# The first MLP layer of the last two token groups in seven products instead of eight, with partial sums in the reopened score banks

## The chip, the cores and the metric

The kernel runs on one core of a Trainium2 chip. The metric is the device time of one execution in microseconds (us); the kernel before takes 329.04 us, the median of three runs (328.96 to 329.2). TensorE is called PE here, its weight loads PEld, VectorE DVE, ScalarE ACT, GpSimd POOL and SyncE SP.

## The reference

Attention with 16 extra keys ("beacons") is followed by a two-layer MLP over its output:

```python
# q, k, v: (8, 8, 576, 64); beacon_k, beacon_v: (8, 8, 16, 64)
scores = q @ concat(beacon_k, k).T / sqrt(64)      # causal over k; the beacons are always seen
a = softmax(scores)
x = (a @ concat(beacon_v, v)).transpose(0, 2, 1, 3).reshape(4608, 512)
h = x @ w_in                                       # 512 -> 2048
g = h / (1 + exp(-1.702 * h))
out = g @ w_out                                    # 2048 -> 512
```

## The kernel before, in words

**Attention.** The 64 pairs of batch and head go in 16 sets of four heads (two sets to a batch). For each set a DVE transpose brings q and k into place (line 418), PE forms scores in chunks of 512 columns for four heads (line 447), which fill one tile of four PSUM banks named s, ACT takes the exponential into a 16-bit tile E (line 458; E has three buffers), POOL or DVE masks (lines 479, 472), DVE sums the exponentials (line 497), PE multiplies E by the values (line 534), and DVE normalises into xT (lines 546 to 569). xT holds the MLP's input transposed: 512 features as four blocks of 128 partitions, by tokens.

**MLP.** The 4608 tokens go in ten groups: two of 256 tokens, then eight of 512 (groups 2 to 9). For a group of 512, the first layer (`e_m1`, line 593) makes 16 tiles of 128 hidden features by 512 tokens. Each tile is four matmuls with 512 columns, summed over the four feature blocks, in one PSUM bank. ACT then takes each tile through the gated activation into a 16-bit tile g (`e_gelu`, line 614). The second layer of groups 2 to 9 already goes by the seven-product scheme (`products`): with 2x2 blocks, seven block products replace eight. DVE makes sums of blocks of g (`e_s`, through `add`, line 658; sixteen operations a group), PE forms the seven products, each 32 matmuls with 256 columns (`e_prod`, line 707), and ACT (`e_half`, line 718) and DVE (`e_join`, line 723, seven a group) put the products together into the output tiles osb, which SP stores (line 730). The weight sums that this needs are made once (`e_t`, line 658, into tB and into a quarter of w2).

**PSUM.** Four of the eight banks belong to s. The other four are a ring, tiles u0 to u3, that serves the value products, the first layer and the second layer. A tile of the ring is free for its next use when the operation that `closes` it has read it.

**Order.** Every piece of work is an operation with an engine, a duration and dependencies, entered by `plan.op`. The order on each engine is written out by hand in the table `ORDER`, as numbers of operations. `Plan.run` walks that table with the entered durations to choose a bank for each ring tile and to merge the engines' orders into one program. On the chip each engine takes its instructions in that order and waits on semaphores, so the entered durations set which bank a tile gets, not when it runs.

Of the kernel before, what the change touches and what calls it, by code (L numbers as in the profile page):

```python
# [10 lines left out]
ALU = mybir.AluOpType  # L11
# [7 lines left out]
        170, 173, 176, 145, 125, 148, 150, 177, 182, 188, 191, 227, 194, 197, 232, 183, 203, 234, 200, 178, 237,  # L19
        179, 206, 258, 241, 209, 184, 263, 185, 212, 265, 213, 248, 246, 268, 214, 215, 401, 251, 253, 272, 218,  # L20
        404, 275, 244, 279, 219, 220, 407, 282, 284, 277, 221, 414, 320, 296, 304, 290, 302, 292, 300, 298, 312,
        308, 294, 318, 314, 310, 306, 316, 426, 435, 423, 343, 338, 339, 340, 433, 431, 438, 344, 345, 359, 349,
        341, 464, 346, 350, 351, 352, 354, 574, 355, 429, 360, 361, 577, 356, 362, 357, 372, 365, 583, 474, 477,
        373, 366, 374, 367, 605, 480, 484, 375, 482, 607, 368, 506, 502, 488, 492, 610, 490, 486, 498, 504, 500,
        508, 514, 510, 516, 494, 496, 512, 534, 593, 596, 535, 536, 539, 540, 550, 541, 542, 537, 742, 545, 546,
        547, 548, 603, 745, 551, 552, 553, 599, 601, 619, 622, 748, 555, 556, 557, 558, 561, 755, 625, 627, 629,
        562, 563, 776, 568, 564, 569, 570, 571, 779, 764, 767, 659, 637, 641, 657, 649, 651, 647, 661, 635, 631,
        653, 805, 772, 770, 774, 643, 655, 633, 639, 645, 679, 680, 815, 818, 700, 681, 682, 684, 701, 915, 690,
        685, 686, 691, 692, 702, 918, 687, 693, 695, 703, 696, 924, 821, 823, 697, 698, 706, 946, 825, 707, 713,
        708, 709, 948, 934, 937, 714, 715, 716, 827, 951, 944, 940, 942, 853, 831, 833, 855, 857, 851, 843, 835,  # L30
        837, 847, 839, 845, 829, 849, 841, 1083, 960, 963, 875, 876, 880, 877, 878, 881, 882, 1086, 968, 966, 970,
        883, 1089, 902, 909, 903, 886, 891, 1096, 887, 888, 889, 892, 893, 1117, 904, 894, 905, 896, 897, 1120, 898,
        899, 910, 911, 1105, 1108, 1146, 912, 976, 994, 996, 972, 978, 1000, 992, 982, 974, 998, 990, 984, 988, 980,
        1002, 986, 1256, 1156, 1113, 1111, 1115, 1159, 1025, 1020, 1026, 1021, 1259, 1022, 1027, 1031, 1023, 1028,
        1265, 1164, 1162, 1166, 1041, 1042, 1287, 1036, 1047, 1032, 1048, 1033, 1037, 1038, 1034, 1039, 1289, 1054,
        1055, 1049, 1056, 1043, 1044, 1050, 1292, 1057, 1198, 1172, 1168, 1178, 1184, 1180, 1194, 1170, 1174, 1176,
        1275, 1278, 1182, 1186, 1196, 1188, 1190, 1281, 1301, 1285, 1283, 1304, 1216, 1217, 1221, 1192, 1222, 1227,
        1218, 1223, 1228, 1219, 1224, 1232, 1229, 1233, 1230, 1307, 1311, 1309, 1237, 1327, 1333, 1238, 1243, 1234,
        1244, 1235, 1323, 1239, 1245, 1250, 1251, 1341, 1240, 1246, 1252, 1253, 1337, 1405, 1315, 1331, 1343, 1411,
        1335, 1321, 1403, 1431, 1313, 1325, 1407, 1419, 1317, 1423, 1425, 1319, 1339, 1421, 1409, 1329, 1361, 1413,  # L40
        1366, 1382, 1429, 1362, 1363, 1401, 1367, 1364, 1427, 1368, 1383, 1372, 1369, 1373, 1374, 1375, 1388, 1377,
        1389, 1378, 1390, 1395, 1379, 1384, 1380, 1385, 1391, 1396, 1415, 1397, 1398, 1470, 1454, 1417, 1455, 1449,
        1471, 1450, 1451, 1476, 1452, 1456, 1477, 1457, 1478, 1460, 1461, 1462, 1463, 1465, 1466, 1467, 1468, 1472,
        1479, 1473, 1483, 1484, 1485, 1486,
# [3 lines left out]
        195, 198, 233, 235, 201, 204, 238, 180, 207, 259, 210, 264, 186, 266, 269, 216, 402, 405, 408, 222, 417,  # L48
        415, 297, 291, 303, 305, 301, 299, 293, 309, 321, 295, 319, 313, 315, 311, 307, 317, 436, 439, 342, 465,
        468, 575, 578, 584, 587, 606, 608, 503, 507, 489, 491, 493, 487, 499, 505, 509, 515, 517, 495, 501, 511,  # L50
        497, 513, 611, 538, 743, 746, 749, 756, 758, 777, 780, 660, 642, 638, 652, 658, 648, 650, 636, 632, 662,
        654, 806, 644, 634, 656, 640, 646, 809, 916, 683, 919, 928, 925, 947, 949, 952, 828, 832, 854, 856, 852,
        858, 834, 838, 844, 840, 836, 846, 830, 848, 850, 842, 1084, 879, 1087, 1090, 1099, 1097, 1118, 1121, 1147,
        1150, 977, 995, 979, 997, 993, 973, 975, 983, 991, 999, 989, 1001, 981, 1003, 985, 987, 1257, 1260, 1024,
        1269, 1266, 1288, 1290, 1293, 1199, 1179, 1173, 1181, 1185, 1195, 1171, 1169, 1175, 1177, 1183, 1187, 1197,
        1189, 1191, 1193, 1220, 1328, 1334, 1324, 1342, 1316, 1332, 1344, 1406, 1412, 1338, 1336, 1404, 1432, 1314,
        1408, 1420, 1318, 1424, 1326, 1426, 1320, 1340, 1422, 1410, 1330, 1322, 1414, 1430, 1402, 1365, 1428, 1416,
        1418, 1453,
# [3 lines left out]
        123, 163, 160, 124, 224, 169, 128, 166, 172, 175, 146, 147, 126, 149, 151, 225, 226, 398, 190, 193, 196,  # L62
        199, 255, 256, 257, 202, 205, 286, 242, 411, 287, 211, 208, 243, 399, 249, 247, 400, 250, 412, 254, 252,
        273, 245, 274, 280, 276, 413, 281, 285, 283, 278, 289, 461, 288, 462, 419, 580, 420, 463, 326, 327, 328,
        421, 322, 92, 323, 324, 422, 427, 428, 424, 425, 325, 330, 334, 329, 335, 432, 336, 331, 434, 337, 332, 333,
        470, 347, 582, 353, 471, 581, 472, 430, 473, 358, 363, 475, 476, 478, 479, 481, 485, 739, 483, 369, 376,
        370, 589, 752, 740, 590, 615, 518, 753, 921, 519, 754, 526, 591, 527, 520, 528, 592, 529, 521, 741, 522,
        597, 523, 594, 530, 595, 598, 531, 802, 532, 524, 533, 616, 543, 525, 604, 549, 617, 618, 554, 600, 620,
        602, 623, 624, 621, 559, 760, 628, 761, 762, 626, 630, 565, 763, 566, 768, 572, 765, 811, 812, 766, 803,
        804, 769, 773, 771, 671, 1080, 775, 672, 813, 922, 663, 814, 664, 675, 667, 816, 673, 819, 668, 669, 817,  # L70
        923, 665, 666, 820, 674, 676, 677, 1093, 670, 688, 694, 678, 930, 822, 824, 699, 931, 826, 932, 933, 704,
        710, 938, 939, 935, 936, 717, 711, 945, 941, 943, 1081, 956, 957, 958, 871, 1082, 1094, 1095, 959, 872, 873,
        867, 859, 961, 962, 964, 965, 860, 863, 1262, 1143, 861, 874, 862, 868, 864, 967, 865, 971, 866, 969, 884,
        869, 870, 1101, 1144, 890, 1145, 1102, 895, 1103, 1104, 900, 906, 1109, 907, 1110, 913, 1106, 1107, 1152,
        1153, 1004, 1154, 1005, 1155, 1264, 1006, 1263, 1016, 1012, 1017, 1157, 1114, 1112, 1013, 1018, 1116, 1160,
        1008, 1161, 1009, 1019, 1158, 1014, 1015, 1029, 1010, 1165, 1011, 1007, 1163, 1167, 1035, 1040, 1271, 1051,
        1045, 1058, 1052, 1297, 1272, 1273, 1274, 1298, 1299, 1276, 1279, 1300, 1200, 1204, 1280, 1201, 1277, 1205,
        1282, 1302, 1206, 1286, 1284, 1208, 1305, 1209, 1202, 1303, 1210, 1212, 1203, 1306, 1207, 1213, 1225, 1231,
        1308, 1312, 1214, 1310, 1215, 1211, 1236, 1247, 1241, 1248, 1254, 1349, 1345, 1350, 1346, 1347, 1353, 1351,
        1354, 1355, 1356, 1357, 1358, 1359, 1370, 1348, 1360, 1352, 1376, 1381, 1386, 1392, 1393, 1445, 1446, 1433,  # L80
        1399, 1437, 1434, 1438, 1447, 1435, 1441, 1442, 1436, 1443, 1444, 1439, 1448, 1440, 1458, 1464, 1469, 1480,
        1474, 1481, 1487,
    ],
    "POOL": [
        8, 10, 12, 14, 16, 17, 19, 21, 23, 25, 27, 29, 31, 33, 35, 37, 39, 41, 43, 45, 47, 110, 49, 51, 113, 114,
        53, 55, 57, 59, 133, 61, 136, 137, 63, 65, 67, 69, 71, 378, 230, 231, 229, 380, 382, 384, 386, 236, 388,
        390, 392, 239, 240, 394, 396, 261, 260, 262, 441, 443, 270, 267, 271, 449, 451, 453, 455, 457, 459, 403,
# [29 lines left out]
class Plan:  # L117
# [6 lines left out]
    def __init__(self, ring):  # L124
        self.ops = []
        self.ring = ring
        self.tiles = {}
        self.closers = {}
# [76 lines left out]
def kernel(  # L205
# [27 lines left out]
    HF = S // 2  # L233
    NKT = DMODEL // P
    NNT = DFF // P
    RING = 4

    NE, NB2, NB3 = 3, 2, 3

# [893 lines left out]
```

## Time and profile before

| what | value |
|---|---|
| time, median of three runs | 329.04 us |
| span of the profiled execution, first to last instruction | 327.2 us |
| around the span (median less span) | 1.8 us |
| mean granted TensorE clock | 0.999 |
| busy: PE, PEld, DVE | 314.6, 214.7, 237.2 us |
| busy: ACT, POOL | 202.1, 113.9 us |
| line 593, first layer: 704 matmuls | 130.6 us |
| line 707, second layer of groups 2 to 9: 896 matmuls | about 121 us |
| line 614, activation of the first layer: 128 | 70.5 us, 598 ns each |

No time of the profiled execution is listed beside its span, so the median of the runs stands in for it: 1.8 us lie around the span. A matmul's busy time overlaps that of the next one, so the time of a run of matmuls is read from start to start. An ACT or DVE instruction likewise overlaps the next one on its engine by some tens of ns to about 0.1 us. An engine's idle time costs nothing unless another engine is waiting for it.

### The profile page before, as it was taken

To read this page: it belongs to the slowest core of one execution; us is meant where nothing else is said; L and a number is where in the kernel's file an instruction comes from. 1 tells how busy PE (TensorE), PEld (TensorE's weight loads), DVE (VectorE), ACT (ScalarE), POOL (GpSimd) and SP (SyncE) were. 2 spreads that over 40 slices of the span, in tenths; PEclk is the share of its full clock that TensorE was granted. 3 is DMA by queue.
4 is the path that set the end of the run, shared out by engine and by line. 5 is a ranking of instruction groups with operands and counts; after the bars stand their busy time and mean duration, and the time that the engine had idled before them with its cause. 6 is when DMAs were issued, how large, how long until landed. Compare 5 with 4: busy or idle time off the path is not lost.

```text
span 327.2 us, 9966 instructions
## 1 busy us (share of the span) xinstructions
PE 314.6 (96%) x4364; PEld 214.7 (66%) x4364; DVE 237.2 (72%) x480; ACT 202.1 (62%) x236; POOL 113.9 (35%) x178
## 2 busy tenths in 40 slices
PE   6589999999999999999999999999999999999995
PEld 6467665545775477746878878547764776447884
DVE  4838798777987989977998798858558853006674
ACT  1676697678767586679666786868577212674010
POOL 8765478190419312941177019400042000000000
PEclk9999999999999999999999999999999999999999
DMA  7999999293424911792039709500120012000122
GB/s 126 159 201 211 204 186 184 37 123 107 99 72 64 190 34 34 79 198 43 7 53 178 119 4 124 154 2 3 34 98 0 2 34 83 15 0 2 65 98 97
DMA packets 58220, 28.83 MB, mean 88 GB/s; under 512 B 41280, under 2 KB 53568, under 8 KB 58176
## 3 DMA queue, kind: packets, MB, share of 16 engines
q0 software_dynamic: 47552, 18.49, 47.9%
q1 hardware_dynamic: 10560, 9.69, 9.2%
q8 instruction: 34, 0.56, 0.7%
q14 instruction: 10, 0.08, 0.1%
q10 hardware_dynamic: 64, 0.01, 0.0%
HBM read 37.22 MB, written 9.44 MB: 143 GB/s over the span
## 4 chain that ended last, share of the span: by engine, by line
PE 83%; DMA 6%; DVE 4%; POOL 3%; ACT 2%; issue 1%; ACTq 0%; POOLq 0%
PE u L593 34%; PE u L707 30%; PE u L534 9%; PE s L447 7%; PE u L638 3%; DMA w<-in_moe_w_out_dram 3%; DMA w<-in_moe_w_in_dram 3%; ACT E L458 1%; DVE sA L658 1%; DVE g L626 1%; POOL vb L378 1%; POOL w L384 0%; DVE bkn L403 0%; ACT L614 0%; DVE kT L418 0%
## 5 line engine op out<-in xcount | busy, mean ns | idle before, releaser
L593 PE MATMUL u<-xT,w 128*128 128x512 f16 (+1 forms) x704 | 130.6, 341 | 0.6 <-ACT g L614 0.5
L458 ACT ACTIVATE E<-s 128x2048 f16<-128x2048 f32 (+5 forms) x66 | 98.9, 1515 | 44.9 <-PE s L447 44.4
L614 ACT ACTIVATE g<-u 128x512 f16<-128x512 f32 x128 | 70.5, 598 | 53.7 <-PE u L593 53.2
L593 PEld LDWEIGHTS <-w 128*128 128x128 f16 x704 | 67.6, 98 | 54.3 <-issue 1.9
L479 POOL TENSOR_SCALAR_AFFINE_SELECT E<-E 128x512 f16<-128x512 f16 (+3 forms) x78 | 49.3, 665 | 110.8 <-ACT E L458 79.1
L723 DVE SCALAR_TENSOR_TENSOR osb<-u,osb 128x512 f32<-128x512 f32 x56 | 37.3, 683 | 24.5 <-PE u L707 22.5
L707 PEld LDWEIGHTS <-g 128*128 128x128 f16 x512 | 48.3, 98 | 9.3 <-issue 0.2
L707 PE MATMUL u<-w,g 128*128 128x256 f16 x384 | 50.6, 273 | 0.0
L447 PE MATMUL s<-qT,kT 32*128 32x32 f16 (+20 forms) x1376 | 34.6, 228 | 5.7 <-ACT E L458 2.8
L447 PEld LDWEIGHTS <-kT 32*128 32x128 f16 x1376 | 25.2, 92 | 22.5 <-issue 14.4
L707 PEld LDWEIGHTS <-sA 128*128 128x128 f16 x384 | 36.3, 98 | 5.3 <-issue 0.3
L707 PE MATMUL u<-tB,sA 128*128 128x256 f16 x256 | 35.1, 273 | 0.1
L658 DVE TENSOR_TENSOR sA<-g 128x512 f16<-128x512 f16 x32 | 12.9, 416 | 26.2 <-ACT g L614 26.2
L569 DVE TENSOR_TENSOR xT<-u,rz 128x352 f16<-128x352 f32 (+2 forms) x52 | 25.5, 517 | 6.5 <-PE u L534 6.3
L378 POOL DMA_DIRECT2D vb<-in_v_dram x32 | 27.4, 876 | 2.4 <-DMA qn<-in_q_dram 1.6
L534 PE MATMUL u<-E,vb 128*32 128x352 f16 (+8 forms) x928 | 27.4, 262 | 0.0
L497 DVE TENSOR_TENSOR zs<-zs,E 128x1344 f16<-128x1344 f16 (+2 forms) x36 | 22.7, 633 | 5.3 <-POOL E L479 4.4
L534 PEld LDWEIGHTS <-vb 128*32 128x32 f16 (+1 forms) x928 | 19.9, 96 | 5.5 <-issue 1.7
L418 DVE STREAM_TRANSPOSE kT<-kn 128x576 f32<-128x576 f32 x16 | 20.1, 1257 | 2.1 <-DMA kn<-in_k_dram 1.4
L418 DVE STREAM_TRANSPOSE qT<-qn 128x576 f32<-128x576 f32 x16 | 19.9, 1241 | 0.3 <-DMA qn<-in_q_dram 0.3
L546 DVE STREAM_TRANSPOSE zt<-u 128x224 f32<-128x224 f32 (+2 forms) x32 | 15.0, 470 | 5.9 <-PE u L534 5.8
L497 DVE TENSOR_TENSOR zs<-E 128x1856 f16<-128x1856 f16 x12 | 15.8, 1320 | 3.3 <-POOL E L479 3.3
(48 smaller groups left out, 252.3 us busy)
## 6 DMA issues: line engine op xcount, KB each, us to landing
out_dram<-osb SPq DMA_DIRECT2D x36, 256.0 KB, 2.4
kn<-in_k_dram POOLq DMA_DIRECT2D x16, 288.0 KB, 6.9
qn<-in_q_dram POOLq DMA_DIRECT2D x16, 288.0 KB, 6.5
vb<-in_v_dram POOLq DMA_DIRECT2D x24, 128.0 KB, 6.4
w<-in_moe_w_in_dram POOLq DMA_DIRECT2D x8, 256.0 KB, 9.4
w<-in_moe_w_out_dram POOLq DMA_DIRECT2D x4, 512.0 KB, 13.5
vb<-in_v_dram POOLq DMA_DIRECT2D x8, 112.0 KB, 5.0
vb<-in_v_dram POOLq DMA_DIRECT2D x8, 80.0 KB, 7.9
```

The lines of the kernel that those rows point to most:

```text
L378: nc.gpsimd.dma_start(out=t[0 : hi - lo, j, h0:h1, :], in_=v[b, h0:h1, lo:hi, :].rearrange("h n d -> n h d"),)
L418: nc.vector.transpose(out=f32(dst.rearrange("p n e -> p (n e)")).rearrange("p (r t) -> p t r", t=TR), in_=f32(src[:, :]).rearrange("p (t c ...
L447: nc.tensor.matmul(sc[:, h, o : o + w], kT[s % NB2][r : r + 32, j * P : (j + 1) * P, d], qT[s % NB2][r : r + 32, a : a + w, d], start=(d = ...
L458: nc.scalar.activation(out=Es[s][:, :, c0:c1], in_=ss[i][:, :, o : o + c1 - c0], func=AFT.Exp, scale=0.125,)
L479: nc.gpsimd.affine_select(out=blk, in_=blk, compare_op=ALU.is_ge, fill=0.0, base=off + (Nb if j == 0 else 0), pattern=[[0, Q], [1, w]], ch ...
L497: nc.vector.tensor_tensor(out=t, in0=E[:, :, Z0:S] if i == 1 else t, in1=E[:, :, wcol[i] : wcol[i] + S - a], op=ALU.add,)
L534: nc.tensor.matmul(u[32 * h : 32 * h + 32, a:e], lhs, src[0:kw, h, col : col + e - a], start=first, stop=last,)
L569: nc.vector.tensor_tensor(out=xT[:, 2 * hs + x : 2 * hs + x + n, t0 : t0 + w], in0=rings[("av", s, x, half)][:, 0 : n * w].rearrange("p (n ...
L593: nc.tensor.matmul(u[:, o + a - t0 : o + e - t0], w1t[:, kp, nt * P : (nt + 1) * P], xT[:, kp, a % XR : (e - 1) % XR + 1], start=(kp == 0) ...
L614: nc.scalar.activation(out=gts[g][:, n0:n1, 0:w], in_=rings[("m1", g, n0)][:, 0 : n * w].rearrange("p (n w) -> p n w", n=n), func=AFT.Gelu ...
L707: nc.tensor.matmul(u[:, HM * mt : HM * (mt + 1)], lhs[:, n, mt * P : (mt + 1) * P], rhs[:, n, :], start=(n == 0 and mt == 0), stop=(n == H ...
L723: nc.vector.scalar_tensor_tensor(out=osbs[(g, dst)][:, :], in0=rings[("p", g, p)][:, :], scalar=scale_of(g), in1=osbs[(g, src)][:, :], op0 ...
```

## The change

The set `FAST = (8, 9)` names the last two groups. Their first layer no longer goes through `e_m1` and `e_gelu`. `fast` cuts the first layer's weights into 2x2 blocks (256 input features by 1024 hidden features) and the group's tokens into two halves of 256, and works in four steps, called tiles here, of twice two blocks of 128 hidden features. A tile has seven parts, each of four matmuls with 256 columns (`e_part`).

- Block sums: four of the weights, made once (`e_ws`, 2048 columns each; three into a buffer of E that is free by then, one into bkf), and four of the tokens for each group (`e_xs`, 512 columns each, into another buffer of E). All eight kinds are DVE additions through `add`.
- The partial sums that several outputs share are not formed in SBUF: ACT copies a bank to another bank (`e_seed`), and the next parts go on summing on top of the copy. Part 1 goes into bank a. Its copy in bank b takes part 6; the copy of that, in bank e, takes part 5. Bank a then takes part 2, bank b part 4, bank e part 3.
- Part 7 goes into bank f, and ACT copies it to SBUF (`e_keep7`, into the buffers qn and kn, which the last transposes have left). DVE adds it to bank e before part 3, and to bank b after part 4 (`e_sum7`), into SBUF.
- ACT takes the four results of a tile through the activation (`e_gelu4`, 512 columns each): two from PSUM, two from SBUF. So a tile has four activations, as before, and three ACT copies and two DVE additions that are new.

PSUM: the pool of s is closed after the last scores and reopened as four tiles of one bank, u4 to u7, so the ring has eight banks from then on, for the remaining work of group 7 and of attention too. The last exponential must have read s first (`late`). A bank that is to be seeded must have been wholly written by its user before (`seeded`, `partial`).

`ORDER` is the same up to about 100 us before the end; from there on PE, ACT, DVE and POOL have a new one, in which operations of attention, of group 7 and of groups 8 and 9 are moved against each other. The dependencies of the second layer are as before, on two activations for each block instead of one.

```diff
-    RING = 4
+    RING, MORE = 4, 4
...
+            else:
+                if not spare:
+                    scoring.close()
+                    spare.append(
+                        ctx.enter_context(tc.tile_pool(name="psv", bufs=1, space=bass.MemoryType.PSUM))
+                    )
+                rings[key] = spare[0].tile([P, 512], F32, tag=f"u{i}", name=f"u{i}")
...
+    FAST = (8, 9)
...
+        for n in range(2):
+            for x in range(2):
+                nc.tensor.matmul(
+                    u[:, HM * n : HM * (n + 1)],
+                    lhs[:, x, (2 * i + n) * P : (2 * i + n + 1) * P],
+                    rhs[:, x, :],
+                    start=fresh and n == 0 and x == 0,
+                    stop=n == 1 and x == 1,
+                    skip_group_check=not fresh,
+                )
+    def e_seed(src, dst):
+        nc.scalar.mul(out=ring_tile(dst)[:, :], in_=rings[src][:, :], mul=1.0)
...
+    def e_keep7(src, slot):
+        nc.scalar.mul(out=hold[slot], in_=rings[src][:, :], mul=1.0)
+
+    def e_sum7(src, slot, dst):
+        nc.vector.tensor_tensor(out=hold[dst], in0=rings[src][:, :], in1=hold[slot], op=ALU.add)
...
+            p1 = part(1, "a", [], True)
+            c1 = grab("seedb", 490, [p1], lambda: e_seed(key["a"], key["b"]), ring=key["b"])
+            p2 = part(2, "a", [c1])
+            gelu(0, 0, p2, key["a"], key["a"])
+            p6 = part(6, "b", [c1])
+            c2 = grab("seede", 490, [p6], lambda: e_seed(key["b"], key["e"]), ring=key["e"])
+            p7 = part(7, "f", [], True)
+            x7 = grab("keep7.", 480, [p7] + last, lambda: e_keep7(key["f"], slots[0]), closes=key["f"])
+            p5 = part(5, "e", [c2])
+            p4 = part(4, "b", [c2])
+            a1 = grab("sum22.", 605, [p5, x7] + last, lambda: e_sum7(key["e"], slots[0], slots[1]), "DVE")
+            g22 = gelu(1, 1, a1, slots[1])
+            p3 = part(3, "e", [a1])
+            gelu(0, 1, p3, key["e"], key["e"])
+            a2 = grab("sum21.", 605, [p4, x7] + last, lambda: e_sum7(key["b"], slots[0], slots[2]), "DVE", closes=key["b"])
+            g21 = gelu(1, 0, a2, slots[2])
...
+        if g in FAST:
+            fast(g, xs, old)
+            products(g)
+            return
```

## The prediction

> **What bounds the kernel now.** I read the page's busy shares first, then the waits of PE from 222 us on, the stretches of the last 100 us, the chain that ended last, and the timeline around one first-layer tile.
>
> ```profile
> PE 314.6 (96%) x4364; PEld 214.7 (66%) x4364; DVE 237.2 (72%) x480; ACT 202.1 (62%) x236; POOL 113.9 (35%) x178
> PEclk9999999999999999999999999999999999999999
> ```
>
> PE is busy for 96% of the span at full clock. A busy PE need not be a limit, so I look for gaps: the waits of PE after 222 us are an empty list, and the stretches say the same.
>
> ```profile
> 225.00:240.00 15.00, 15.00 (x263) 12.08 (x264) 8.79 (x21) 8.49 (x7) 1.83 (x3) 1.00 0.06 20
> 240.00:265.00 25.00, 25.00 (x301) 15.27 (x300) 19.34 (x43) 12.77 (x19) 4.73 (x7) 1.00 0.13 44
> 265.00:324.00 59.00, 58.38 (x416) 39.76 (x408) 25.40 (x56) 19.55 (x34) 0.00 (x0) 1.00 0.11 40
> ```
>
> The columns are length, then PE, PEld, DVE, ACT and POOL busy, clock, DMA. PE has no idle time from 225 us to its last matmul near 323.4. From 265 us on, where groups 8 and 9 lie, DVE works 25.4 of 59 us and ACT 19.6, so there is room for more work on both. The chain confirms that only PE's own work stands between there and the end:
>
> ```profile
> 274.75 18.99 PE u L593 x88
> ...
> 300.26 8.30 PE u L707 x76
> ...
> 323.42 0.69 DVE osb L723
> ```
>
> These two rows are the prices. A matmul of 512 columns in a run costs 18.99 / 88 = 215.8 ns, one of 256 columns, with its own weight load, 8.30 / 76 = 109.2 ns. After the last matmul come a join, a store and the end of the program.
>
> **What PE loses.** A group's first layer is 64 matmuls of 512 columns: 64 x 215.8 = 13.81 us. After the change it is 4 tiles x 7 parts x 4 = 112 of 256 columns: 112 x 109.2 = 12.23 us. That is 1.58 us a group, **3.16 us** for two. In the two programs' orders of instructions I find these and no other matmuls changed, and as many changes between scores, values and whole-array matmuls as before (16 after 225 us). Each part lasts 0.437 us.
>
> The row for 256 columns comes from operands like the new ones (16-bit, 128x128 weights from SBUF). The Trainium skill, "TensorE: Matmul & The Clock Gate", section "Back-to-back issue gap", speaks against the change: in a stream of load and matmul pairs it gives about 81 ns for 128 columns and 131 ns for 512. Estimated on a line between, 256 columns cost 98 ns, and a group would go from 64 x 131 = 8.4 to 112 x 98 = 10.9 us, 2.6 us more. This case's trace disagrees, with 215.8 and 109.2 ns.
>
> **What ACT and DVE gain.** ACT: as many activations, plus 8 tiles x 3 copies = 24 of 128x512. The rows of that size (line 614, 598 ns; line 718, 597) agree whatever the function; back to back one costs 0.49 us (below). So 24 x 0.49 to 0.60 = 11.8 to 14.4 us, and ACT has 31 to 34 of some 56 us. Sixteen copies write PSUM, and no row shows ACT doing that. The low bound is a write with no fixed part: the exponentials of line 458 take 1877 ns for 2048 columns and 1452 for 1536, so 512 columns alone cost 0.43 us. The high bound is twice the row, 1.20. I take 0.60, the row of the same shape, which differs only in the destination.
>
> DVE: 4 weight sums of 2048 columns, where the row for tB (line 658) has 1214 ns twice and 1695 once: 4.9 to 6.8 us. They fall between 240 and 265, where DVE has 5.7 us idle, 6.2 more from 225 on, and the new order brings three sums of exponentials (633 ns each) forward into the earlier stretch and puts two normalisations (517 ns) after 265. That makes 19.3 + 4.9 - 0.6 x 3 - 1.0 = 21.4 of 25 us, 23.3 at the dear price. It stays under cover. What is late next is the last normalisation of set 15, which the first part of group 8 needs; the fourth weight sum stands just before it. If the cover is gone, 0.5 us a sum, at most 2 us. After 265: 8 token sums (0.34 to 0.42 us) and 16 additions of part 7 (as line 723's 128x512 from PSUM: 0.61 to 0.69), 12.5 to 14.4 us on 25.4, some 39 of 56.
>
> DMAs, SP's order and POOL's work stay; on POOL only masks change places, and it is idle 10 of 15 us there. Six more waits stand on PE, most for beacon loads that landed long ago: a wait instruction lasts 51 ns in the trace, so 0 to 0.3 us. The one between 250 and 255 us left no gap in PE, so I take zero.
>
> **The new waits.** PE runs in order: behind a part that waits for a copy, every later matmul stands, those of the second layer too. What a link costs:
>
> ```profile
> 311.00 1.03 PE L593 MATMUL u<-xT,w 128*128 128x512 f16 x4
> 311.86 1.04 PE L707 MATMUL u<-w,g 128*128 128x256 f16 x8
> 312.06 0.60 ACT L614 ACTIVATE g<-u 128x512 f16<-128x512 f32 x1 [2.01 <-PE u L593]
> ```
> ```profile
> 68.87 1.08 ACT L614 ACTIVATE g<-u 128x512 f16<-128x512 f32 x2
> 69.52 0.59 PE L593 MATMUL u<-xT,w 128*128 128x512 f16 x2 [0.49 <-ACT g L614]
> ```
>
> ACT starts 0.20 us after PE goes on to the next run. In the second view two activations take 1.08, so the second follows at 0.49; the first ends at 69.47 and PE starts at 69.52, 0.05 later. A link PE, ACT, PE is 0.20 + 0.60 + 0.05 = 0.85 us, two parts (0.87). Over DVE it is 0.20 + 0.69 + 0.05 = 0.94. In the new order at least three parts (1.31 us) stand between the two ends of every link: exactly three in 6 of the 40, four or more in the rest. What can still hurt is ACT's own queue: one instruction ahead costs 0.49. I followed the order with these prices through the stretches with least room. The copy of bank b for tile 3 of group 8 must await the part-7 addition of tile 2, which frees its bank: 0.20 + 0.69 + 0.03 + 0.60 + 0.05 = 1.57 us, and four parts (1.75) cover it, 0.18 to spare. The copy into e for tile 2 stands behind an activation that comes late: 0.20 + 0.49 + 0.60 + 0.05 = 1.34 against 1.75. I find none under 0.1. The bound on the dear side: 6 close links x 0.5 = 3 us. I take zero, because each link has been counted.
>
> Eight banks in place of four give nothing: PE had no gap to remove.
>
> **The rivals.**
> 1. **Forecast: PE's work falls and nothing takes its place.** 329.04 - 3.16 = **325.9 us**, span 324.0. Chance 0.70.
> 2. **Waits in the chains or on DVE's weight sums eat part.** ACT copying at 0.8 instead of 0.6 would use up the tightest 0.18, and a few tenths at some five links make 1 to 2 us: 326.9 to 327.9. Against it: the counted margins. Chance 0.17.
> 3. **Slower: copies into PSUM are dear, and PE waits for ACT.** Place: the 16 seeds. With d for one, and some 0.2 us of room on average, the loss is 16 x (d - 0.8): it decides from d = 1.0 us (16 x 0.2 = 3.2), and at the bound of 1.20 it makes 6.4, 332.3 us. For it: no row shows such a write. Against it: the row does not depend on what is written (f16 598, f32 597). Chance 0.09. The Trainium skill, "ScalarE: Activation LUTs", section "Step-by-step: what each stage is for", has ScalarE's writes to PSUM faster than to SBUF; no run here shows it, and by that rule this rival has no chance.
> 4. **Narrow matmuls are bound by their weight loads.** A load is 98 ns busy, a pair 109.2: if the new sources make a pair 123.3 ns, 112 x 123.3 = 13.81 and the gain is gone; one after the other, 98 + 107 = 205 ns, two groups lose 224 x 96 = 21 us, 347. Against it: line 707 runs 896 such pairs with no gap. Chance 0.02; the page on TensorE above is this rival's rule in its milder form, plus 5.2 us.
> 5. **The change doesn't do what it says**: of the two groups only group 8 saves, because in group 9 PE runs short of ready work near the end, where its second layer needs all activations: 329.04 - 1.58 = 327.5. Against it: in the new order 22 product parts (9.6 us) stand behind the last first-layer part, about as now. Chance 0.02.
>
> **How the numbers follow.** Faster by over 0.2% (0.66 us, about what a measurement of this kernel can tell from no change) holds for 1, most of 2 and 5: 0.70 + 0.14 + 0.02 = 0.86. Within 0.2%: 0.03 of 2 and 0.01 of 3, 0.04. Slower: 0.08 of 3 and 4's 0.02, 0.10. The range: 325.3 (0.6 below the forecast for the spread of runs and a price read a little off) to 327.4, which takes in the six waits at 0.3 and losses to 1.5 us, the nearer part of rival 2: 0.68 of case 1 and 0.12 of case 2. The dear bounds (2 us of weight sums, 3 of links, rivals 3 to 5) lie beyond it, with the 0.2 that is left.
>
> **What would show it.** Right: the span 324.0, PE without waits after 225 us, 224 matmuls of 256 columns at 109 ns from start to start, ACT near 33 and DVE near 39 us busy in the last 56. Wrong: PE waiting for the copies (rival 2 or 3), their mean above 0.8 us, or DVE's weight sums running past set 15's normalisation.

## The result, and the profile after

The changed kernel takes **326.18 us** (median of five runs, 325.29 to 326.32) against 329.2 us for the kernel before (five runs, 328.96 to 329.44). The ratio is 0.9906, with a 95% interval of 0.9894 to 0.9918: 3.02 us less. The forecast was 325.9, in a range of 325.3 to 327.4.

The page of the profile after, first the busy shares and the granted clock:

```profile
PE 310.6 (96%) x4460; PEld 223.6 (69%) x4460; DVE 253.2 (78%) x508; ACT 213.7 (66%) x260; POOL 114.1 (35%) x178
...
PEclk9999999999999999999999999999999999999999
```

PE's share stays at 96% and the span is 323.6 us. ACT has 11.6 us more work and DVE 16.0 us more, and PE 4.0 us less. The stretches of the last 100 us, with the columns as before (length, PE, PEld, DVE, ACT, POOL, clock, DMA):

```profile
225.00:240.00 15.00, 15.00 (x282) 11.91 (x276) 9.65 (x21) 9.83 (x7) 3.09 (x5) 1.00 0.06 21
240.00:265.00 25.00, 25.00 (x280) 15.74 (x278) 20.39 (x42) 10.56 (x19) 3.06 (x4) 1.00 0.09 33
265.00:320.00 55.00, 54.40 (x508) 48.36 (x496) 39.99 (x82) 31.76 (x58) 0.00 (x0) 1.00 0.14 48
```

PE is still without a gap until its last matmul. In the last stretch DVE is at 40.0 of 55 us, where it was at 25.4 of 59, ACT at 31.8, where it was at 19.6, and the weight loads fill 48.4. The list of PE's waits after 222 us is empty, as it was. The chain that ended last, from 265 us on (start, length, what):

```profile
270.06 3.49 PE u L813 x32
...
309.79 3.51 PE u L724 x32
313.32 0.60 ACT osb L735
313.93 1.64 issue
315.56 0.70 DVE osb L740
316.35 0.70 DVE osb L740
317.12 0.70 DVE osb L740
317.85 1.35 DVE osb L740 x3
```

Two things are to be seen. A matmul of the new parts costs 3.49 / 32 = 109.1 ns. And the chain no longer ends in PE's last matmul and one join. It leaves PE at 313.3 and ends in a row of DVE's joins. The 1.64 us of "issue" between them are a wait for which the profile names nobody; e8 below shows that it is a wait for PE.

**Where the time went.** Up to about 224 us both kernels issue the same matmuls in the same order, so the start of the matmul that follows the 3300th can serve as a mark in every trace. It divides a span into a part that the change does not touch, the stretch from there to the start of the last matmul, and the end.

| kernel | mark at | from it to the start of the last matmul | from there to the end |
|---|---|---|---|
| before | 221.68 us | 101.43 us | 4.11 us |
| after | 220.96 | 98.17 | 4.46 |
| e1, before with eight banks | 221.98 | 101.32 | 4.11 |
| e2, part 7 twice | 221.45 | 101.66 | 4.47 |
| e3, copies twice | 221.46 | 102.56 | 4.46 |
| e4, weight sums twice | 221.41 | 98.81 | 4.46 |
| e5, copies longer | 221.91 | 98.71 | 4.46 |
| e6, additions twice | 221.80 | 104.53 | 4.46 |
| e7, half of each part | 221.90 | 93.00 | 4.47 |
| e8, one step of the order moved | 221.73 | 98.17 | 4.15 |
| e9, after again | 221.99 | 98.17 | 4.47 |
| e10, e8 again | 223.51 | 98.17 | 4.15 |

The spans differ by 3.6 us (327.2 and 323.6), but 0.72 of that arose in the untouched part, in the first 50 us of it; over all traces that part scatters from 220.96 to 223.51. What the change did is in the other two columns: 3.26 us less in the stretch, 0.35 us more at the end, 2.91 in all. The medians say 3.02.

### The profile page after: what moved, and what is told of

Same layout as the page of the kernel before. It is cut to its first block, busy times and chain, and to the rows that moved or that the text cites. A ratio compares the mean times of both kernels' runs of the same rounds, so it can differ in the third digit from the quotient of the medians.

```text
span 323.6 us, 10241 instructions
## 1 busy us (share of the span) xinstructions
PE 310.6 (96%) x4460; PEld 223.6 (69%) x4460; DVE 253.2 (78%) x508; ACT 213.7 (66%) x260; POOL 114.1 (35%) x178
## 4 chain that ended last, share of the span: by engine, by line
PE 83%; DMA 6%; ACT 3%; POOL 3%; DVE 3%; issue 1%; DVEq 0%; ACTq 0%; POOLq 0%
PE u L724 28%; PE u L610 27%; PE u L551 9%; PE s L464 8%; PE u L813 8%; PE u L655 4%; DMA w<-in_moe_w_out_dram 3%; DMA w<-in_moe_w_in_dram 2%; ACT E L475 2%; DVE osb L740 1%; DVE sA L675 1%; POOL vb L395 1%; POOL w L401 0%; ACT L631 0%; POOL kn L379 0%
## 5 line engine op out<-in xcount | busy, mean ns | idle before, releaser
L610 PE MATMUL u<-xT,w 128*128 128x512 f16 (+1 forms) x576 | 101.9, 332 | 1.1 <-DVE xT L586 0.6
L610 PEld LDWEIGHTS <-w 128*128 128x128 f16 x576 | 55.0, 98 | 41.0 <-issue 2.1
L631 ACT ACTIVATE g<-u 128x512 f16<-128x512 f32 x96 | 51.7, 599 | 21.4 <-PE u L610 21.1
L724 PEld LDWEIGHTS <-g 128*128 128x128 f16 x512 | 48.4, 98 | 7.1 <-issue 0.2
```

Source lines behind the costliest of these rows:

```text
L610: nc.tensor.matmul(u[:, o + a - t0 : o + e - t0], w1t[:, kp, nt * P : (nt + 1) * P], xT[:, kp, a % XR : (e - 1) % XR + 1], start=(kp == 0) ...
L631: nc.scalar.activation(out=gts[g][:, n0:n1, 0:w], in_=rings[("m1", g, n0)][:, 0 : n * w].rearrange("p (n w) -> p n w", n=n), func=AFT.Gelu ...
L724: nc.tensor.matmul(u[:, HM * mt : HM * (mt + 1)], lhs[:, n, mt * P : (mt + 1) * P], rhs[:, n, :], start=(n == 0 and mt == 0), stop=(n == H ...
```

## The experiments

**e1: the banks alone.** The kernel before with its own order, and the score banks reopened as four ring tiles.

```diff
-    FAST = (8, 9)
+    FAST = ()
```
(and `ORDER` of the kernel before in the changed kernel)

> The kernel before, with its own order, but with the score banks reopened as four more tiles of the ring; both layers of all groups as before. Theory 1 (the change gained only the matmul time of the first layer, 3.16 us): PE had no gap after 225 us in the profile of before, so more banks give nothing: within 0.3 us of before. Theory 2 (part of the gain is that PE and ACT no longer share four banks): 1 to 3 us faster than before.

329.09 us against 329.09 of before measured beside it, ratio 1.0002 (0.9992 to 1.0011). The banks alone give nothing that the time can show. The stretch became 0.11 us shorter: in the trace of before, one first-layer matmul at 244.5 starts 0.10 us late, while it waits for its bank, and with eight banks it does not. That gap does not show in the list of waits.

**e2: eight parts instead of seven.**

```diff
-  lambda: e_part(g, p, i, key[at], fresh)
+  lambda: [e_part(g, p, i, key[at], fresh) for _ in range(2 if p == 7 else 1)]
```

> The changed kernel with part 7 formed twice in each of the eight tiles (the second overwrites the first, the result is the same): eight parts instead of seven, 256 matmuls of 256 columns in the two groups instead of 224. Theory 1 (PE's work sets the time): 8 x 4 x 109.2 ns = 3.5 us slower than the changed kernel, 0.3 to 0.5 us slower than before. Theory 2 (banks and order carry part of the gain): as slow, but then faster than before by what they carry, 1 us or more. Theory 3 (ACT or DVE sets the time of these groups): less than 2 us slower than the changed kernel, since PE then has idle time to fill.

329.36 us, ratio to before 1.0013 (1.0003 to 1.0023). The stretch grew by 3.49 us, which is 32 x 109.1 ns. With the eighth product given back, nothing of the gain is left. Against e1, which has the same eight banks, the stretch is 0.34 us longer, and 256 matmuls of 256 columns should take 256 x 109.1 - 128 x 215.8 ns = 0.31 us more than 128 of 512. So in the stretch the new order, the copies and the additions cost PE at most some 0.03 us; what they do cost is the 0.36 at the end. Theory 1 holds, and 2 and 3 fall.

**e3: each copy from bank to bank twice.**

```diff
-        nc.scalar.mul(out=ring_tile(dst)[:, :], in_=rings[src][:, :], mul=1.0)
+        for _ in range(2):
+            nc.scalar.mul(out=ring_tile(dst)[:, :], in_=rings[src][:, :], mul=1.0)
```

> The changed kernel with each of the 16 copies from bank to bank done twice, which adds 0.49 us of ACT to each. Theory 1 (each link between PE and ACT has only some tenths of a us to spare: 0.2 to 0.5 in the tightest places that were counted): the spare time is used up at about ten places and PE waits 0.1 to 0.5 us at each: 2 to 3 us slower than the changed kernel. Rival of the prediction (little to spare, loss of 16 x (d - 0.8) with d = 1.09): 4.6 us slower. Theory 3 (ACT has much room: 32 of 55 us busy): under 0.5 us slower.

330.47 us, ratio 1.0044 (1.0027 to 1.0060): 4.3 us slower than the changed kernel and slower than before. Theory 3 falls. The two other numbers can't be taken as they stand, because the edit added more than 0.49 us to a copy. The first copy from bank to bank, alone in the changed kernel and twice here:

```profile
268.18 0.58 ACT L823 ACTIVATE u<-u 128x512 f32<-128x512 f32 x1 [5.25 <-DVE osb L740]
```
```profile
268.68 1.20 ACT L824 ACTIVATE u<-u 128x512 f32<-128x512 f32 x2 [5.25 <-DVE osb L740]
```

In all 16 pairs the second copy starts 0.61 to 0.65 us after the first, when the first has ended, and not 0.49 after it: a pair takes 1.2 us. For that the rival's rule says 16 x (1.2 - 0.8) = 6.4 us, so its 4.6 came near the measured 4.3 by luck. PE's waits in that kernel:

```profile
PE u L813 <- ACT u L824: 2.7, 8, 0.5
```

The list counts from the modelled end of the matmul before, some 0.16 us after the next could have started. Counted against the same matmuls of the changed kernel, ten new parts start 0.18 to 0.68 us late, 4.4 us in all. In the changed kernel the ten have 0.19 to 0.43 us to spare, and 0.62 less what each has makes 3.1 us. At six of them that agrees with their delay to 0.02. The other four come 0.56 to 0.68 us late instead of 0.21 to 0.37. ACT's timeline shows why at one of them (start, length, operation, count), first in the changed kernel, then here:

```profile
269.70 1.14 ACT L823 ACTIVATE u<-u 128x512 f32<-128x512 f32 x2 [0.95 <-PE u L813]
270.76 0.59 ACT L837 ACTIVATE g<-u 128x512 f16<-128x512 f32 x1
```
```profile
270.61 2.30 ACT L824 ACTIVATE u<-u 128x512 f32<-128x512 f32 x4 [0.73 <-PE u L813]
272.82 0.59 ACT L838 ACTIVATE g<-u 128x512 f16<-128x512 f32 x1
```

Two copies stand one behind the other, so the second bears its own lengthening and that of the first: from the start of the first to the end of the second 2.30 us pass instead of 1.14. The part that needs the second copy had 0.31 us to spare and meets 1.16, not 0.62. Of the 0.85 that are left, 0.18 show at the part that needs the first copy and 0.67 at this one. At the other three it is not shown which lengthening ACT's queue still carried.

**e4: each weight sum twice.**

```diff
-  lambda i=i: e_ws(i)
+  lambda i=i: [e_ws(i) for _ in range(2)]
```

> The changed kernel with each of the four weight sums done twice: 4.9 us more of DVE between 240 and 265 us, where it is busy 20.4 of 25 us. Theory 1 (the sums lie in DVE's idle time, which ends with one set of normalisations): DVE is just full, and PE waits up to 1 us: 0.5 to 1.2 us slower than the changed kernel. Rival (the sums already stand in the way of attention's last normalisations): the whole 4.9 us shows, or more than 2.

326.48 us, ratio 0.9924 (0.9907 to 0.9940), 0.3 us slower than the changed kernel by the medians, 0.64 by the stretch. All of it is at the place that was named, the first parts of group 8 waiting for attention's last normalisation (the second wait, 0.13 us, is below the list's limit):

```profile
PE u L813 <- DVE xT L586: 0.4, 1, 0.4
```

So 5.0 us more of DVE's work (each second sum starts 1.22 to 1.25 us after the first) cost 0.64: the weight sums do lie under cover. The rival falls.

**e5: each copy some tenths longer.**

```diff
+        for w in (64, 512):
+            nc.scalar.mul(out=ring_tile(dst)[:, 0:w], in_=rings[src][:, 0:w], mul=1.0)
```

> The changed kernel with a copy of the first 64 columns ahead of each of the 16 copies from bank to bank, so that each costs ACT some 0.1 to 0.2 us more (0.17 us of fixed part, of which about 0.1 overlaps). In the trace of the changed kernel the shortest time from the end of a copy to the matmul that needs it is 0.24 us, of which 0.05 is the handover. Theory 1 (0.2 us to spare at the tightest link, and the loss of 4.4 us with a whole second copy came from spare time being used up): under 0.3 us slower than the changed kernel. Rival (links have no spare time, and each tenth of a us at a copy shows): 16 x 0.1 to 0.2 = 1.6 to 3.2 us slower.

326.68 us, ratio 0.9926 (0.9911 to 0.9941); 0.5 us slower, 0.54 by the stretch. The full copy starts 0.24 to 0.28 us after the short one, so a copy became 0.25 us longer and not 0.1 to 0.2; ACT's busy time in the last stretch rose by less, from 31.8 to 34.6 us, 0.18 a copy. The loss lies between the two theories and much nearer the first: five links ran out of spare time, by 0.03 to 0.19 us. Together with e3 the price of a copy is a curve: 0.25 us more on each costs 0.5 in all, 0.62 more costs 4.4.

**e6: each addition of part 7 twice.**

```diff
+        for _ in range(2):
             nc.vector.tensor_tensor(out=hold[dst], in0=rings[src][:, :], in1=hold[slot], op=ALU.add)
```

> The changed kernel with each of the 16 additions of part 7 done twice: 16 x 0.61 = 9.8 us more of DVE in the last 56 us, where it is busy 40. Theory 1 (links over DVE have 0.25 to 1.3 us to spare, and DVE's last sums follow each other closely): 3 to 5 us slower than the changed kernel. Rival (DVE has room, 50 of 56): under 1 us slower.

332.63 us, ratio 1.0113 (1.0096 to 1.0129): 6.45 us slower, 6.36 by the stretch, more than was expected. PE's waits:

```profile
PE u L813 <- DVE kn L832: 2.0, 3, 0.7
PE u L813 <- DVE qn L832: 1.2, 3, 0.6
PE u L813 <- ACT u L823: 1.1, 2, 0.6
PE u L724 <- DVE kn L832: 0.2, 1, 0.2
```

PE waits for DVE, and for ACT as well, which itself waits for the additions (its activations 12.3 us, against 4.3 in the changed kernel, and its copies 0.8). A second addition starts 0.71 to 0.73 us after the first, not 0.61, so 11.5 us were put on DVE. More than half of them show, though DVE's share rises only to 44.8 of 55 us. Room in the busy share is not room in the chain.

**e7: half of each part left out.**

```diff
-            for x in range(2):
+            for x in range(1):
...
-                    stop=n == 1 and x == 1,
+                    stop=n == 1,
```

> The changed kernel with only one of the two input blocks in each part, so half the matmuls of the seven parts are left out (112 of 224, 12.2 us of PE); the output is then not the reference's. It asks what is late next. Theory 1 (DVE with 40 us of work in what would be 43, and the chains of copies, come next): PE waits, and the time falls by 6 to 10 us instead of 12.2. Rival (PE alone still sets the time): 12 us faster than the changed kernel.

321.03 us, ratio 0.9757 (0.9738 to 0.9777): 5.15 us faster than the changed kernel, though 12.2 us of PE's work are gone. That is less than theory 1 said, and its mechanism holds:

```profile
PE u L813 <- ACT u L823: 2.6, 6, 0.5
PE u L813 <- DVE qn L831: 1.0, 2, 0.7
PE u L724 <- ACT g L837: 0.2, 1, 0.2
```

PE starts late 20 times, 7.1 us in all; the list shows the longer ones, from modelled ends. In this order, what comes next after PE is the chain of copies and additions, some 5 us below the present time. The parts that cover the links are halved here too, so with whole parts that bound may lie lower; no run shows it.

**e8: one step of PE's order moved.** The last quarter of product 2 of group 9 (operation 1533) moves up four places, to stand behind operation 1528.

```diff
-        1527, 1530, 1531, 1548, 1532, 1528, 1538, 1542, 1553, 1549, 1533, 1539, 1543, ...
+        1527, 1530, 1531, 1548, 1532, 1528, 1533, 1538, 1542, 1553, 1549, 1539, 1543, ...
```

> The changed kernel with one step of PE's order moved: the last quarter of product 2 of group 9 stands four steps earlier, so that DVE can begin the seven joins of group 9 some 1.6 us earlier. In the trace of the changed kernel the last join starts 0.25 us after the last matmul has ended, behind six others in a row, where it started 0.04 after it before the change. Theory 1 (the joins in a row hold the end up): the last join starts 0.04 after the last matmul, and the program ends 0.2 us earlier, about 0.06%. Rival (stores or the end of the program hold it up): the end stays where it is.

325.66 us, ratio 0.9894 (0.9880 to 0.9909). DVE's timeline at the end, in the changed kernel and here:

```profile
312.84 0.75 DVE L675 TENSOR_TENSOR g<-g 128x512 f16<-128x512 f16 x2
315.56 4.77 DVE L740 SCALAR_TENSOR_TENSOR osb<-u,osb 128x512 f32<-128x512 f32 x7 [1.97 <-issue]
```
```profile
314.72 0.69 DVE L740 SCALAR_TENSOR_TENSOR osb<-u,osb 128x512 f32<-128x512 f32 x1 [0.36 <-ACT osb L735]
316.71 0.69 DVE L740 SCALAR_TENSOR_TENSOR osb<-u,osb 128x512 f32<-128x512 f32 x1 [1.30 <-PE u L724]
317.58 3.31 DVE L740 SCALAR_TENSOR_TENSOR osb<-u,osb 128x512 f32<-128x512 f32 x5 [0.18 <-PE u L724]
```

In the first, the first join waits 1.97 us, and then seven follow one another. The profile names nobody for that wait, but with product 2's last quarter moved and nothing else, the first join starts 1.6 us earlier after the mark (at 92.99 instead of 94.60 us). So that quarter is what it waited for. In the second, two joins are done early. The end after the last matmul shrinks from 4.46 to 4.15 us, nearly the 4.11 of before, and the stretch stays. Theory 1 holds, with 0.3 us instead of 0.2.

**e9 and e10: the changed kernel and e8, again, beside each other.**

> The changed kernel as it is, beside e10 on one chip. Both theories: 3.0 us faster than before (0.991), the last matmul 98.2 us after matmul 3300 and 4.45 us before the end.

> The kernel of e8 again, beside e9 on one chip. Theory 1 (the joins in a row hold the end up by 0.3 us): 0.3 us faster than e9 (0.990 of before), the last matmul 98.2 us after matmul 3300 and 4.15 us before the end. Rival (the 0.5 us between the medians of e8 and of the changed kernel were of the chip and the day): the same time as e9.

e9 326.26 us, ratio 0.9903 (0.9889 to 0.9917); e10 325.97 us, 0.9898 (0.9880 to 0.9917). The medians differ by 0.29 us, as the traces say (4.47 and 4.15), but the intervals overlap: the times alone do not prove a tenth of a per cent. In the traces the end is 4.46 and 4.47 us in the two of the changed kernel and 4.15 in both of the moved order.

## Why the prediction was right

- **The sum.** 3.16 us of matmul time was forecast. The stretch of e1 and that of the changed kernel, with the same eight banks, differ by 101.32 - 98.17 = 3.15 us, and e2 gives it back at 109.1 ns a matmul. The six added waits on PE, taken at zero, leave no trace in it. By the rule of the Trainium skill ("TensorE: Matmul & The Clock Gate", section "Back-to-back issue gap") that was weighed against the row, 256 columns would cost an estimated 98 ns and the change would lose. The trace disagrees, with 109.1 ns.
- **ACT's copies** were taken at 0.60 us and measure 0.59, so the high bound of 1.20 did not occur, and with it rival 3. The rival's rule, 16 x (d - 0.8), holds near its edge: e5 has d = 0.83, for which it says 0.5 us, and 0.5 were measured. Further out it is too dear: e3 has d = 1.2, for which it says 6.4, and 4.4 were measured, because only ten of the 16 copies delay a part. That a copy at the high bound makes the kernel slower than before, as the rival said, is so: e3 has that d.
- **The links.** The tightest was counted at 0.18 us to spare. In the trace of after the shortest time from the end of a copy to the matmul that needs it is 0.24, of which 0.05 is the handover: 0.19. It is the link that was named: its copy starts at 283.05, after the addition that ends at 283.01. No wait arose. What failed is how fast the room goes once it is gone (expected 2 to 3 us in e3). One part of that is the edit, which added 0.62 us and not 0.49; the other is that links were counted one by one, which gives 3.1 us of the 4.4, and ACT's queue carries lateness on.
- **DVE's weight sums** measure 1183 to 1219 ns, the low end of their price, and the cover that was named (idle time up to set 15's last normalisation) is the one that e4 used up.
- **Eight banks give nothing**: 0.11 us, one gap that the list of waits does not show. The step said that PE had no gap to remove; it had one of a tenth.
- **What the sum left out** is the end. The prediction read there a last join and a store, as before. The new order finishes product 2 of group 9 late, the joins bunch on DVE, and the end grew by 0.35 us: the last join starts 0.22 later after the last matmul, and 0.13 are added behind it. e8 takes 0.31 of that back. With the end, 3.15 + 0.11 - 0.35 = 2.91 us; the forecast of 3.16 was 0.14 larger than the 3.02 of the medians. That the 0.11 and the 0.35, neither of which the sum had, partly cancel is luck. The rest of the distance between 325.9 and 326.18 is that the forecast started from 329.04, and before took 329.2 beside the result. Rival 5 looked at that place for PE, where nothing happened, and not for DVE.
- Rival 2 did not occur, and nor did 4: at 109.1 ns a pair the loads stayed hidden, with PEld at 48.4 of 55 us.

## What to carry to other kernels

Where one engine is without a gap to the end, as PE is here, a change that takes work from it is worth that work at the row's price, and the question is only whether the work given to the others stays hidden. Answer it by links rather than by busy shares: for each place where the full engine needs a result, set what is queued between the two ends against the handover, the operation and what stands before it in that engine's queue. Look at the last few microseconds separately, because an order that keeps the full engine full can still leave the others a row of work behind it. And where an experiment does an instruction twice, read from its trace how much that added, before its time is held against a rule.

## What the runs showed of the hardware

The groups of ACT's work in the last 60 us of the changed kernel (line, operation, shapes, count, busy us and mean ns, idle before and releaser):

```profile
L837 ACT ACTIVATE g<-u 128x512 f16<-128x512 f32 x16 | 9.5, 592 | 3.1 <-PE u L813 2.3 <-DVE g L675 0.7
L823 ACT ACTIVATE u<-u 128x512 f32<-128x512 f32 x16 | 9.4, 589 | 7.8 <-DVE osb L740 5.3 <-PE u L813 2.3
L837 ACT ACTIVATE g<-kn 128x512 f16<-128x512 f32 x8 | 5.0, 626 | 2.0 <-DVE kn L831 2.0
L837 ACT ACTIVATE g<-qn 128x512 f16<-128x512 f32 x8 | 4.9, 628 | 2.4 <-DVE qn L831 2.3
L828 ACT ACTIVATE qn<-u 128x512 f32<-128x512 f32 x4 | 2.4, 597 | 1.3 <-PE u L813 1.3
L828 ACT ACTIVATE kn<-u 128x512 f32<-128x512 f32 x4 | 2.4, 594 | 0.6 <-PE u L813 0.5
```

These means mix instructions that start on an idle ACT with some that overlap the one before. Of those alone that start after idle time, the same activation takes 597 ns from PSUM and 629 to 630 from SBUF: the source costs 33 ns. A copy to PSUM takes 582 ns and one to SBUF 597: the destination costs 15. The Trainium skill ("ScalarE: Activation LUTs", section "Step-by-step: what each stage is for") has writes to PSUM faster than to SBUF; the trace agrees, by 2.5%.

A second copy into the same bank starts 0.03 us after the first has ended (e3, e5), while an activation behind a copy in the queue starts 0.49 after the copy's start, before it has ended. In the same way a second addition into the same tile starts 0.71 to 0.73 us after the first (e6), where the addition of another result follows at 0.61 (six times in e6). No run shows why.

The stretch of 98.17 us is the same to 0.01 us in four traces with the same work on PE (after, e8, e9, e10), while the part before it scatters by 2.5 us. What scatter there is from run to run arises in the first 50 us; no run shows its cause.
